# A fixed TensorE order from the second block on, and the first block's weight pairs behind the exponentials, in a windowed attention and two MLPs

## The chip, the cores and the metric

The kernel runs on one NeuronCore of a Trainium2 chip. The metric is the device time of one execution in microseconds. The runs of the kernel before took 1015.44, 1015.37 and 1014.34 us, median 1015.37.

Names used below: PE is TensorE (PEld its weight loads), ACT is ScalarE, DVE is VectorE, POOL is GpSimd, SP is SyncE, whose queue issues the DMAs.

## What is computed

```python
# q, k, v: (4, 8, 576, 64)
scores = scale * np.matmul(q, k.transpose(0, 1, 3, 2))
rel = pos[:, None] - pos[None, :]
mask = (rel >= 0) & (rel < 64)
attn = softmax(where(mask, scores, -1e9))       # in float32
x = np.matmul(attn, v)                          # -> (2304, 512) by token
xn = x / np.sqrt(np.mean(x * x, -1, keepdims=True) + 1e-6) * rms_g
g = xn @ w_gate                                 # 512 -> 1536
x = (g * sigmoid(g) * (xn @ w_val)) @ w_out     # 1536 -> 512
h = x @ w_in                                    # 512 -> 2048
out = (h * sigmoid(1.702 * h)) @ w_out2         # 2048 -> 512
```

## The kernel before

The 2304 tokens are six blocks of 384; a block is three attention tiles of 128 tokens, numbered 0 to 17. A tile is worked on in steps: `att_Tk` and `att_Tq` transpose K and Q on PE and copy them to SBUF; `att_S` computes the scores into two PSUM banks, DVE adds the mask and takes the row minimum, ACT takes eight exponentials, DVE normalises; `att_PT` transposes P; `att_PV` multiplies with V. `rms_sq` squares the result and adds its four parts on DVE, `rms_sum` sums over the partitions on PE and takes the power on POOL, `rms_spread` spreads it on PE and scales x on DVE. `split_x` splits x into two fp32r numbers, `xh` and `xl`.

A projection (`proj`) is twelve matmuls: weight high half by `xh`, low half by `xh`, high half by `xl`, four contraction chunks each. Weights come by DMA as float32 into staging tiles (`st`, three buffers) and are converted pair by pair: `w_step` runs two operations on ACT (lines 163 and 164), then three on DVE (165, 166, 169) that build a rounded number m; `w_half`, at the next step, casts m to the high half on ACT (144) and subtracts on DVE for the low half (145). A pair holds the gate and value weights of one feature chunk, or the output weights of two. The first pass over the six blocks uses the first six feature chunks (nine pairs, 0 to 8), all converted during block 0; the second pass the other six; the second MLP follows.

The opening works off tiles 0 to 2 alone. It has its own PSUM banks and SBUF tiles, and five matmuls of the identity after each transpose (`ps_warm`). Then block 0 begins, and the steps of the later tiles are put between its matmuls: `tick()` counts the matmuls of the projections and accumulations (216 per block), and `due` holds what is to be issued at which count, from the table `score_at` (tile 3 at tick 10, then 42, 74, 112, 202, and every 72).

A scheduler orders each engine's instructions at build time. Where `pinned[0]` is set, PE's instructions keep the order in which the code issues them (`tc.keep_in_program_order`); before, this holds for all blocks of the first pass. `tc.issue_after(ins)` keeps an instruction behind another. `hold[0]` is such an instruction for the two ACT operations of a weight pair: in the opening the last copy, then the split of x, from block 1 on the latest tanh.

The feature loop (lines 601 to 641) runs, per chunk: gate projection, tanh (607) and product (610), value projection, product (614), cast `ah` (617), difference `al` (618), and the accumulation of the chunk before (`emit_O`). `extras` calls `w_step` between them.

Of the kernel before, what the change touches and what calls it, by code (L numbers as in the profile page):

```python
# [22 lines left out]
def window_attention__gated_mlp__mlp_kernel(  # L23
# [28 lines left out]
    T0 = TB  # L52
# [83 lines left out]
    def after(ins):  # L136
        return tc.issue_after(ins) if ins is not None else nullcontext()

    def w_half():
        if not half:  # L140
            return
        pair, w24 = half.pop()
        w = wp.tile([128, 2, 1024], F32R, tag="w", name="w")
        nc.scalar.copy(w[:, 0, :], w24.bitcast(F32))
        nc.vector.tensor_tensor(w[:, 1, :], w24.bitcast(F32), w[:, 0, :].bitcast(F32), ALU.subtract)
        for e, key in enumerate(pair):
            weights[key] = w[:, :, e * 512:(e + 1) * 512]

    def w_step(limit):
        w_half()  # L150
        if w_next[1] >= min(limit, n_w):
            return
        w_load(w_next[1] + 1)
        pair = w_order[w_next[1]]
        w_next[1] += 1
        st = staged.pop(0).rearrange("p e (f two) -> p (e f) two", two=2)
        lo, hi = st[:, :, 0], st[:, :, 1]
        if w_next[1] <= n_wh:
            m = wp.tile([128, 1024], I32, tag="w", name="m")
        else:  # L160
            m = tmp.tile([128, 1024], I32, tag="tmp", name="m")
        with after(hold[0]):
            nc.scalar.mul(hi.bitcast(F32), hi.bitcast(F32), 2.0 ** -112)
            nc.scalar.activation(lo, lo.bitcast(U32), AF.Copy, scale=2.0 ** -29)
        nc.vector.tensor_scalar(m.bitcast(U32), hi.bitcast(U32), 3, None, ALU.logical_shift_left)
        nc.vector.scalar_tensor_tensor(
            m.bitcast(U32), hi.bitcast(U32), 0x80000000, m.bitcast(U32), ALU.bitwise_and, ALU.bitwise_or
        )
        nc.vector.tensor_tensor(m, m, lo, ALU.add)
        half.append((pair, m))  # L170
        w_load(w_next[1] + 2)
# [78 lines left out]

    last_copy = [None]

    def to_sbuf(dst, src, vector=False):
        if vector:
            nc.vector.tensor_copy(dst, src)
        else:
            last_copy[0] = nc.scalar.copy(dst, src).ins

    def att_Tk(m):
        t = ld_tile["k", m]  # L260
        ps = att_bank("k")
        for hp in range(NHP):
            on_pe(nc.tensor.transpose, ps[:, hp * 128:(hp + 1) * 128], t[:, 2 * hp:2 * hp + 2, :], ident)
        s0 = 2 * (m % 2)
        to_sbuf(KT[:, :, s0:s0 + 2, :], ps.rearrange("p (h g t) -> p h g t", h=NHP, g=2), starting[0] and m > 0)
        released(("k", m))

    def att_Tq(m):
# [7 lines left out]
        qts[m] = QT  # L276
        to_sbuf(QT, ps.rearrange("p (h t) -> p h t", h=NHP))
        released(("q", m))
# [9 lines left out]
    def att_S(m):  # L288
# [22 lines left out]
        for e in range(2):  # L311
# [12 lines left out]
            for hp in range(NHP):  # L324
                i = e * NHP + hp
                last_exp[0] = nc.scalar.activation(  # L326
                    p[e][:, hp, :],
                    p[e][:, hp, :],
                    AF.Exp,
                    bias=sm[:, 0, i:i + 1],  # L330
                    scale=-1.0,
                    accum_out=sm[:, 1, i:i + 1],
                ).ins
        for lo, n, pe in [(0, NHP, p[0]), (NHP, NHP, p[1])] if starting[0] else [(0, 2 * NHP, pp)]:
            r = sm[:, 2, lo:lo + n]
# [56 lines left out]
    def rms_sum(x, sq, lo, hi):  # L392
# [24 lines left out]

    def rms_scale(x, sq, lo, hi):
        rms_sum(x, sq, lo, hi)
        return rms_spread(x, lo, hi)  # L420
# [64 lines left out]


    N_ATT = NG // 2
    m0 = TB // 128
    score_at = [0] * m0 + [10, 42, 74, 112] + [202 + 72 * i for i in range(N_ATT - 2 * m0)]

    for fn in (att_Tk, att_Tq):
        at_tick(1, lambda fn=fn: held(fn, m0))
    for m in range(m0, N_ATT):
        b, i = divmod(m, m0)
        t, n = score_at[m], score_at[m + 1] - score_at[m]
        if m == m0:
            at_tick(t, lambda m=m: held(att_S, m))
        else:
            at_tick(t, lambda m=m: att_S(m))
# [4 lines left out]
        at_tick(t + (60 if i == 0 and b > 1 else 48) * n // 72, lambda m=m: att_PT(m, (1,)))  # L504
        pv = t + n + 10
        at_tick(pv, lambda m=m, b=b, i=i: att_PV(m, x_of(b)[0], i * 128))
        at_tick(pv, lambda b=b, i=i: rms_sq(x_of(b)[0], i * 128, x_of(b)[1]))
        if i + 1 == m0:
            at_tick(pv + 24, lambda b=b: rms_sum(*x_of(b), 0, TB))
            at_tick(pv + 38, lambda b=b: rms_spread(x_of(b)[0], 0, TB))  # L510

    if True:
# [52 lines left out]
        for ps_i in range(2):  # L565
            f_lo, f_hi = ps_i * FH, (ps_i + 1) * FH
            for j in range(NB):
                end = j + 1 == NB
                pinned[0] = ps_i == 0
                acc = [acc_p.tile([128, 512], F32, tag=f"acc{c}", name=f"acc{c}") for c in range(KC)]  # L570
# [30 lines left out]
                for f in range(f_lo, f_hi):  # L601
# [14 lines left out]
                    al = ap_.tile([128, TB], F32R, tag="al", name="al")  # L616
                    nc.scalar.copy(ah, a)  # L617
                    nc.vector.tensor_tensor(al, a, ah.bitcast(F32), ALU.subtract)  # L618
# [121 lines left out]
```

## Time and profile before

| what | value |
|---|---|
| median of 3 runs | 1015.37 us |
| the profiled execution's own time | 1013.77 us |
| its span in the profile | 1012.0 us |
| mean granted clock of TensorE | 0.984 |
| PE busy | 975.2 us, 96% |
| DVE, ACT, POOL busy | 51%, 40%, 1% |
| HBM read and written | 68.55 MB and 18.87 MB |

The span is what the profile shows, from the first to the last recorded event; the time is 1.8 us longer. All times in the rows are counted from the start of the span. Busy PE says little of its pace: the granted clock of a stretch (1.00 is 2.4 GHz, 0.50 is 1.2 GHz) has to be read with it.

### The profile page before, as it was taken

Reading aid. Unit: us, or ns where it says so; the run is one execution under the profiler, and the core shown is the slowest. Engines: PE = TensorE matmul, PEld = TensorE weight load, DVE = VectorE, ACT = ScalarE, POOL = GpSimd, SP = SyncE. Lnnn points to the kernel's source line nnn. Section 1 sums busy time; section 2 is a strip of 40 time slices with the busy share of each in tenths; the row PEclk is TensorE's granted clock in tenths of the full one; section 3 lists DMA queues with packets and bytes.
Section 4 is the critical chain, followed back from the end, with each engine's and each line's share of the span. In section 5 each row is a group of like instructions: output and inputs, shape, how many; then the busy total and the mean of one; then the engine's idle time right before and its main releaser. Section 6 shows DMA issues by size and latency. Waiting matters only on the chain.

```text
span 1012.0 us, 15556 instructions
## 1 busy us (share of the span) xinstructions
PE 975.2 (96%) x6200; PEld 914.3 (90%) x6200; DVE 518.6 (51%) x1140; ACT 404.9 (40%) x882; POOL 12.5 (1%) x39
## 2 busy tenths in 40 slices
PE   8569999999999999999999999999999999999997
PEld 7458999989999899999999998998989989989996
DVE  5896657667676654564552788232332322322222
ACT  6687455646563333332332464232222222322222
POOL 2000000000000000000000000000000000000000
PEclk9779999999999999999999999999999999999999
DMA  9866443636443422433421442010010100000000
GB/s 234 215 208 162 112 118 79 175 92 157 116 115 107 158 86 78 136 99 121 135 96 41 136 157 73 1 63 1 1 63 1 45 19 1 32 1 1 32 1 32
DMA packets 113321, 88.44 MB, mean 87 GB/s; under 512 B 77664, under 2 KB 104288, under 8 KB 113248
## 3 DMA queue, kind: packets, MB, share of 16 engines
q1 hardware_dynamic: 112720, 87.44, 29.9%
q8 instruction: 49, 0.80, 0.3%
q14 instruction: 24, 0.20, 0.1%
q10 hardware_dynamic: 528, 0.00, 0.0%
HBM read 68.55 MB, written 18.87 MB: 86 GB/s over the span
## 4 chain that ended last, share of the span: by engine, by line
PE 92%; ACT 2%; DMA 2%; DVE 2%; issue 1%; SPq 0%; POOL 0%; ACTq 0%; DVEq 0%
PE psh L91 20%; PE acc L667 20%; PE acc L91 15%; PE psg L91 14%; PE psv L91 14%; PE ps_v L91 2%; PE ps_s L91 2%; PE ps_t L91 2%; DMA st<-in_moe_w_out_dram 1%; ACT p L326 1%; PE ps_r L91 1%; PE ps_q L91 1%; PE ps_warm L91 1%; PE ps_k L91 1%; DMA o<-x2s 1%
## 5 line engine op out<-in xcount | busy, mean ns | idle before, releaser
L683 DVE TENSOR_TENSOR a<-a,psh 128x384 f32<-128x384 f32 x96 | 53.0, 553 | 202.1 <-ACT a L682 202.1
L91 PE MATMUL psh<-x2h,w 128*128 128x384 f32 x768 | 153.2, 339 | 0.0
L667 PE MATMUL acc<-w,gh 128*128 128x512 f32 x576 | 152.8, 397 | 0.0
L91 PEld LDWEIGHTS psh<-x2h,w 128*128 128x128 f32 x768 | 137.2, 188 | 3.2 <-DVE a L683 0.4
L682 ACT ACTIVATE a<-psh 128x384 f32<-128x384 f32 x96 | 47.0, 491 | 220.4 <-PE psh L91 217.2
L667 PEld LDWEIGHTS acc<-w,gh 128*128 128x128 f32 x576 | 107.0, 188 | 18.5
L91 PE MATMUL acc<-ah,w 128*128 128x384 f32 x576 | 116.4, 342 | 1.9 <-ACT ah L617 1.5
L91 PEld LDWEIGHTS acc<-ah,w 128*128 128x128 f32 x576 | 102.1, 188 | 2.8 <-ACT ah L617 1.8
L91 PE MATMUL psh<-x2l,w 128*128 128x384 f32 x384 | 86.2, 338 | 0.0
L667 PE MATMUL acc<-w,gl 128*128 128x512 f32 x288 | 85.1, 396 | 0.0
L610 DVE SCALAR_TENSOR_TENSOR a<-a,psg 128x384 f32<-128x384 f32 x72 | 39.6, 550 | 83.6 <-ACT a L607 83.6
L687 DVE TENSOR_TENSOR gl<-a,gh 128x384 fp32r<-128x384 f32 x96 | 53.4, 557 | 50.5 <-ACT gh L686 42.7
L607 ACT ACTIVATE a<-psg 128x384 f32<-128x384 f32 x72 | 35.4, 491 | 103.3 <-PE psg L91 103.3
L91 PEld LDWEIGHTS psh<-x2l,w 128*128 128x128 f32 x384 | 69.9, 188 | 5.9
L686 ACT CAST gh<-a 128x384 fp32r<-128x384 f32 x96 | 49.3, 513 | 62.4 <-DVE a L683 49.7
L91 PE MATMUL acc<-al,w 128*128 128x384 f32 x288 | 67.5, 348 | 1.5 <-DVE al L618 1.5
L617 ACT CAST ah<-a 128x384 fp32r<-128x384 f32 x72 | 37.0, 513 | 76.2 <-DVE a L614 75.9
L667 PEld LDWEIGHTS acc<-w,gl 128*128 128x128 f32 x288 | 54.2, 189 | 12.5
L91 PE MATMUL psg<-xh,w 128*128 128x384 f32 x288 | 63.7, 354 | 1.5 <-ACT xh L427 1.5
L326 ACT ACTIVATE p<-p,sm 128x128 f32<-128x128 f32 x128 | 49.6, 389 | 29.0 <-DVE sm L314 29.0
L91 PE MATMUL psv<-xh,w 128*128 128x384 f32 x288 | 60.8, 351 | 0.0
L91 PE MATMUL psv<-x2h,w 128*128 128x384 f32 x288 | 58.9, 340 | 0.0
(108 smaller groups left out, 1415.1 us busy)
## 6 DMA issues: line engine op xcount, KB each, us to landing
st<-in_moe_w_out_dram SPq DMA_DIRECT2D x28, 512.0 KB, 4.3
o<-x2s SPq DMA_DIRECT2D x48, 192.0 KB, 3.8
st<-in_moe_w_in_dram SPq DMA_DIRECT2D x16, 512.0 KB, 4.9
st<-in_moe_w_gate_dram SPq DMA_DIRECT2D x12, 512.0 KB, 4.1
st<-in_moe_w_val_dram SPq DMA_DIRECT2D x12, 512.0 KB, 5.2
qkv<-in_v_dram SPq DMA_DIRECT2D x20, 256.0 KB, 4.0
x<-xraw SPq DMA_DIRECT2D x6, 768.0 KB, 3.3
xr<-x SPq DMA_DIRECT2D x6, 768.0 KB, 4.3
```

Source lines behind the costliest of these rows:

```text
L91: ins = op(*args, **kw)
L326: last_exp[0] = nc.scalar.activation(p[e][:, hp, :], p[e][:, hp, :], AF.Exp, bias=sm[:, 0, i:i + 1], scale=-1.0, accum_out=sm[:, 1, i:i + ...
L607: tanh = nc.scalar.activation(a, psg[:, :T], AF.Tanh, scale=0.5).ins
L610: nc.vector.scalar_tensor_tensor(a, a, 1.0, psg[:, :T], ALU.add, ALU.mult)
L617: nc.scalar.copy(ah, a)
L667: nc.tensor.matmul(acc[c], (gh, gh, gl)[pi][:, c * 128:(c + 1) * 128], w[:, (0, 1, 0)[pi], :], start=(f == 0 and pi == 0), stop=(f == NF2 ...
L682: nc.scalar.activation(a[:, :T], psh[:, :T], AF.Sigmoid, scale=1.702)
L683: nc.vector.tensor_tensor(a[:, :T], a[:, :T], psh[:, :T], ALU.mult)
L686: nc.scalar.copy(gh[:, :T], a[:, :T])
L687: nc.vector.tensor_tensor(gl[:, :T], a[:, :T], gh[:, :T].bitcast(F32), ALU.subtract)
```

## The change

It has these parts:

- `pinned[0]` is set only from block 1 on (`j > 0`), so in block 0 the scheduler orders PE. The tiles 3 to 5 of block 0 are no longer issued at ticks but at `slots`, the calls of `extras` (three per feature chunk); tile 6 and later stay at ticks, from 220 on, at first 48 apart. The normalisation of a block follows its last tile sooner (18 and 30 ticks instead of 24 and 38).
- Weight pairs 1 and 2 wait on ACT for the copy of tile 3's Q, pairs 3 and 4 for tile 3's last exponential, 5 and 6 for tile 4's, 7 and 8 for tile 5's (`gates`, whose key is the pair's number plus one).
- In the opening pair 0 is converted right behind tile 2's last exponential, each operation in two halves of 512 columns.
- In the opening the four parts of the squares are added by PE (four matmuls per tile) instead of two additions on DVE, and each tile is normalised as soon as it is done. K's copies, two of which were DVE's, are all ACT's.
- The split of the next block's input stands behind the last chunk's `ah` and `al`.

```diff
+    def w_cols():
+        return [slice(0, 512), slice(512, 1024)] if starting[0] else [slice(0, 1024)]
...
-        nc.scalar.copy(w[:, 0, :], w24.bitcast(F32))
-        nc.vector.tensor_tensor(w[:, 1, :], w24.bitcast(F32), w[:, 0, :].bitcast(F32), ALU.subtract)
+        for c in w_cols():
+            nc.scalar.copy(w[:, 0, c], w24[:, c].bitcast(F32))
+            nc.vector.tensor_tensor(w[:, 1, c], w24[:, c].bitcast(F32), w[:, 0, c].bitcast(F32), ALU.subtract)
...
-        with after(hold[0]):
-            nc.scalar.mul(hi.bitcast(F32), hi.bitcast(F32), 2.0 ** -112)
-            nc.scalar.activation(lo, lo.bitcast(U32), AF.Copy, scale=2.0 ** -29)
+        for c in w_cols():
+            h, l, mc = hi[:, c], lo[:, c], m[:, c]
+            with after(gates.get(w_next[1], hold[0])):
+                nc.scalar.mul(h.bitcast(F32), h.bitcast(F32), 2.0 ** -112)
+                nc.scalar.activation(l, l.bitcast(U32), AF.Copy, scale=2.0 ** -29)
...
-        to_sbuf(KT[:, :, s0:s0 + 2, :], ps.rearrange("p (h g t) -> p h g t", h=NHP, g=2), starting[0] and m > 0)
+        to_sbuf(KT[:, :, s0:s0 + 2, :], ps.rearrange("p (h g t) -> p h g t", h=NHP, g=2))
...
+        ins = to_sbuf(QT, ps.rearrange("p (h t) -> p h t", h=NHP))
+        if m == T0 // 128:
+            gates[2] = gates[3] = ins
...
+        if 0 <= m - T0 // 128 < 3:
+            for i in range(2):
+                gates[2 * (m - T0 // 128) + 4 + i] = last_exp[0]
...
+        if starting[0]:
+            return s4
...
-            on_pe(nc.tensor.matmul, ms[:, i:i + 1], sq[:, c0:c0 + 128], ones, start=True, stop=True)
+            parts = [sq[:, c0:c0 + 128]] if s4 is None else [s4[:, c, :] for c in range(KC)]
+            for c, part in enumerate(parts):
+                on_pe(nc.tensor.matmul, ms[:, i:i + 1], part, ones, start=(c == 0), stop=(c == len(parts) - 1))
...
-    score_at = [0] * m0 + [10, 42, 74, 112] + [202 + 72 * i for i in range(N_ATT - 2 * m0)]
+    score_at = [220, 268, 316, 364, 433, 502, 572, 642, 712, 784, 856, 928, 1000]
...
+        s0, lags = 1 + 4 * i, (2, 3, 4, 5, 5, 6)
...
+    at_slot(0, s0 + lags[5], lambda: rms_sum(*x_of(1), 0, TB))
+    for fn in (att_Tk, att_Tq):
+        at_slot(0, s0 + lags[5], lambda fn=fn: fn(2 * m0))
+    at_slot(0, s0 + lags[5], lambda: rms_spread(x_of(1)[0], 0, TB))
...
-            at_tick(pv + 24, lambda b=b: rms_sum(*x_of(b), 0, TB))
-            at_tick(pv + 38, lambda b=b: rms_spread(x_of(b)[0], 0, TB))
+            at_tick(pv + 18, lambda b=b: rms_sum(*x_of(b), 0, TB))
+            at_tick(pv + 30, lambda b=b: rms_spread(x_of(b)[0], 0, TB))
...
+        hold[0] = last_exp[0]
+        w_step(1)
         ps_warm = [acc_p.tile([128, 512], F32, tag="acc3", name="ps_warm")]
         for m in range(T0 // 128):
             att_PT(m)
-            if m + 1 == T0 // 128:
-                hold[0] = last_copy[0]
-                w_step(1)
             att_PV(m, x, m * 128)
-            rms_sq(x, m * 128, sq)
-        for m in range(T0 // 128):
-            pe_hold = rms_scale(x, sq, m * 128, (m + 1) * 128)
+            s4 = rms_sq(x, m * 128, sq)
+            pe_hold = rms_scale(x, sq, m * 128, (m + 1) * 128, s4)
+        w_half()
...
-                pinned[0] = ps_i == 0
+                pinned[0] = ps_i == 0 and j > 0
...
-                        split_x(x, nxh, nxl, T)
+                        with after(ah_ins), after(al_ins):
+                            split_x(x, nxh, nxl, T)
```

Three places in the order of instructions. ACT, start of block 0, before (`st` are the staged pairs 1 to 3, `KT` and `QT` the copies of tile 3's K and Q):

```order
L427 CAST xh_552<-xraw_215 128x384 x2
L163 ACTIVATE st_117<-st_117 128x1024
L164 ACTIVATE st_117<-st_117 128x1024
L163 ACTIVATE st_122<-st_122 128x1024
L164 ACTIVATE st_122<-st_122 128x1024
L163 ACTIVATE st_577<-st_577 128x1024
L164 ACTIVATE st_577<-st_577 128x1024
L257 COPY KT_93<-ps_k_582 128x4x128
L257 COPY QT_92<-ps_q_590 128x512
```

The same place in the changed kernel:

```order
L438 CAST xh_565<-xraw_215 128x384
L259 COPY KT_93<-ps_k_597 128x4x128
L438 CAST xh_565<-xraw_215 128x384
L259 COPY QT_92<-ps_q_605 128x512
L169 ACTIVATE st_117<-st_117 128x1024
L170 ACTIVATE st_117<-st_117 128x1024
L169 ACTIVATE st_122<-st_122 128x1024
L170 ACTIVATE st_122<-st_122 128x1024
L148 CAST w_679<-m_613 128x1024
```

Tile 3's copies moved in front of all pairs of block 0, and pair 3 behind pairs 1 and 2.

ACT around tile 4's exponentials (`p_798`), with the pairs 5 (`st_750`) and 6 (`st_827`) and chunk 2's tanh (line 639), in the changed kernel:

```order
L330 ACTIVATE p_798,sm_797<-p_798,sm_797 128x128 x8
L169 ACTIVATE st_750<-st_750 128x1024
L170 ACTIVATE st_750<-st_750 128x1024
L169 ACTIVATE st_827<-st_827 128x1024
L639 ACTIVATE a_843<-psg_830 128x384
L170 ACTIVATE st_827<-st_827 128x1024
L381 COPY xraw_846<-ps_v_848 128x4x128
```

Before, there stood (tile 4's exponentials, `p_765`, behind the first operations of the pair `st_1028`; `a_736` is chunk 1's):

```order
L144 CAST w_1019<-m_899 128x1024
L607 ACTIVATE a_736<-psg_709 128x384
L163 ACTIVATE st_1028<-st_1028 128x1024
L164 ACTIVATE st_1028<-st_1028 128x1024
L144 CAST w_1118<-m_1022 128x1024
L326 ACTIVATE p_765,sm_764<-p_765,sm_764 128x128 x8
L257 COPY KT_93<-ps_k_791 128x4x128
```

The pairs moved from ahead of a tile's exponentials to behind them, and a tanh came to stand behind weight operations.

PE, the spread of the normalisation for block 1 (`ps_r<-ident,ry`), before, in the middle of block 0:

```order
L91 MATMUL acc_566<-ah,w 128x384
L91 MATMUL acc_567<-ah,w 128x384
L91 MATMUL ps_r<-ident,ry 128x128 x3
L91 MATMUL acc_564<-ah,w 128x384
L91 MATMUL acc_565<-ah,w 128x384
```

In the changed kernel, at the end of block 0:

```order
L91 MATMUL acc_577<-al,w 128x384
L91 MATMUL acc_578<-al,w 128x384
L91 MATMUL acc_579<-al,w 128x384
L91 MATMUL acc_580<-al,w 128x384
L91 MATMUL ps_r<-ident,ry 128x128 x3
L91 MATMUL psg<-xh,w 128x384 x4
L91 MATMUL ps_s<-KT,QT 64x128 x16
```

The spread moved behind the last accumulation of block 0, directly in front of block 1's first projection.

## Rows read from the trace of the kernel before

**Rows 1.** The page: the span, and busy time of the engines.

```profile
span 1012.0 us, 15556 instructions
PE 975.2 (96%) x6200; PEld 914.3 (90%) x6200; DVE 518.6 (51%) x1140; ACT 404.9 (40%) x882; POOL 12.5 (1%) x39
```

**Rows 2.** Stretches: length, busy time per engine (instructions); PE's clock, DMA share, GB/s.

```profile
21.90:38.17 16.27, 9.43 (x108) 8.13 (x108) 10.36 (x28) 8.51 (x15) 1.99 (x3) 0.84 0.85 212
38.17:80.00 41.83, 27.04 (x185) 23.91 (x186) 39.83 (x80) 36.32 (x69) 0.00 (x0) 0.70 0.78 219
80.00:122.45 42.45, 42.44 (x405) 39.22 (x405) 26.56 (x89) 23.55 (x76) 0.86 (x1) 0.99 0.45 120
122.45:175.60 53.15, 52.10 (x468) 49.45 (x467) 34.55 (x103) 28.83 (x80) 0.85 (x1) 1.00 0.45 110
```

**Rows 3.** Waits of PE, 38.1 to 80 us: total, times, longest.

```profile
PE ps_t L91 <- DVE p L338: 4.7, 1, 4.7
...
PE ps_q L91 <- ACT KT L257: 3.2, 1, 3.2
PE ps_s L91 <- ACT QT L257: 2.5, 1, 2.5
```

**Rows 4.** Timeline, opening's end: start, length, engine, operation, [idle before <- releaser].

```profile
29.71 0.63 ACT L386 ACTIVATE quad<-xraw 128x512 f32<-128x512 f32 x1
...
32.85 0.80 PE L91 MATMUL ps_r<-ones,sq 128*128 128x1 f32 x4 [3.40 <-DVE sq L388]
...
36.20 2.15 DVE L413 SCALAR_TENSOR_TENSOR xraw<-xraw,g_sb,ps_r 128x128 f32<-128x128 f32 x8 [1.47 <-PE ps_r L91]
...
38.17 0.69 PE L91 MATMUL psg<-xh,w 128*128 128x384 f32 x1 [1.49 <-ACT xh L427]
```

**Rows 5.** Timeline of PE around the end of block 0.

```profile
117.55 1.10 PE L91 MATMUL ps_s<-KT,QT 64*64 64x128 f32 x32
118.58 0.62 PE L91 MATMUL acc<-al,w 128*128 128x384 f32 x2
...
120.55 1.15 PE L91 MATMUL ps_v<-pt,qkv 128*64 128x64 f32 x32
121.63 0.98 PE L91 MATMUL acc<-al,w 128*128 128x384 f32 x4
122.45 0.60 PE L91 MATMUL ps_k<-ident,qkv 128*128 128x128 f32 x4
122.80 1.66 PE L91 MATMUL psg<-xh,w 128*128 128x384 f32 x8
...
125.00 0.60 PE L91 MATMUL ps_q<-ident,qkv 128*128 128x128 f32 x4
```

**Rows 6.** Groups by shape, 36.7 to 122.5 us: busy, mean ns, idle before.

```profile
L166 DVE SCALAR_TENSOR_TENSOR m<-st,m 128x1024 uint32<-128x1024 uint32 x8 | 9.8, 1222 | 0.1
...
L145 DVE TENSOR_TENSOR w<-m,w 128x1024 fp32r<-128x1024 f32 x8 | 9.7, 1214 | 0.5 <-ACT w L144 0.5
...
L314 DVE CUSTOM_DVE_ANT_0 p<-ps_s,masks 128x128 f32<-128x128 f32 x40 | 8.8, 286 | 0.7 <-PE ps_s L91 0.7
...
L165 DVE TENSOR_SCALAR m<-st 128x1024 uint32<-128x1024 uint32 x8 | 5.5, 690 | 0.0
...
L338 DVE TENSOR_TENSOR p<-p,sm 128x1024 f32<-128x1024 f32 x4 | 4.9, 1218 | 0.0
...
L614 DVE TENSOR_TENSOR a<-a,psv 128x384 f32<-128x384 f32 x6 | 3.3, 550 | 2.3 <-PE psv L91 2.3
...
L413 DVE SCALAR_TENSOR_TENSOR xraw<-xraw,g_sb,ps_r 128x384 f32<-128x384 f32 x4 | 2.2, 608 | 0.0
```

**Rows 7.** Timeline of DVE: the low half of pair 8.

```profile
84.50 1.23 DVE L145 TENSOR_TENSOR w<-m,w 128x1024 fp32r<-128x1024 f32 x1 [0.45 <-ACT w L144]
```

**Rows 8.** Short stretches: length, PE busy; PE's clock, DMA share, GB/s.

```profile
72.20:74.70 2.50, 2.47 (x40) 1.00 0.99 329
77.80:80.70 2.90, 2.81 (x10) 0.50 1.24 251
```

**Rows 9.** Timeline of PE ahead of the first of them.

```profile
71.89 0.63 PE L91 MATMUL ps_k<-ident,qkv 128*128 128x128 f32 x4 [1.56 <-issue]
```

More of the change, by code (lines that the diff above doesn't have):

```diff
@@ L161, in w_step @@
             m = tmp.tile([128, 1024], I32, tag="tmp", name="m")
-        with after(hold[0]):
-            nc.scalar.mul(hi.bitcast(F32), hi.bitcast(F32), 2.0 ** -112)
-            nc.scalar.activation(lo, lo.bitcast(U32), AF.Copy, scale=2.0 ** -29)
[L165 to L169, printed above, removed]
+        for c in w_cols():
[3 more added lines that the diff above has]
+                nc.scalar.activation(l, l.bitcast(U32), AF.Copy, scale=2.0 ** -29)
+            nc.vector.tensor_scalar(mc.bitcast(U32), h.bitcast(U32), 3, None, ALU.logical_shift_left)
+            nc.vector.scalar_tensor_tensor(
+                mc.bitcast(U32), h.bitcast(U32), 0x80000000, mc.bitcast(U32), ALU.bitwise_and, ALU.bitwise_or
+            )
+            nc.vector.tensor_tensor(mc, mc, l, ALU.add)
         half.append((pair, m))
@@ L232, in window_attention__gated_mlp__mlp_kernel @@
     hold = [None]
+    gates = {}
     starting = [True]
@@ L249, in att_bank, with to_sbuf @@
         return atp.tile(shape, F32, tag="att", name="ps_" + kind)
[L251 to L257, printed above, removed]
+    def to_sbuf(dst, src):
+        return nc.scalar.copy(dst, src).ins
     def att_Tk(m):
@@ L276, in att_Tq @@
         qts[m] = QT
-        to_sbuf(QT, ps.rearrange("p (h t) -> p h t", h=NHP))
+        ins = to_sbuf(QT, ps.rearrange("p (h t) -> p h t", h=NHP))
+        if m == T0 // 128:
+            gates[2] = gates[3] = ins
         released(("q", m))
@@ L390, in window_attention__gated_mlp__mlp_kernel, with rms_sum @@
     rms_r = {}
-    def rms_sum(x, sq, lo, hi):
+    def rms_sum(x, sq, lo, hi, s4=None):
         n = (hi - lo) // 128
@@ L416, in rms_spread, with rms_scale @@
         return mm.ins
-    def rms_scale(x, sq, lo, hi):
-        rms_sum(x, sq, lo, hi)
+    def rms_scale(x, sq, lo, hi, s4=None):
+        rms_sum(x, sq, lo, hi, s4)
         return rms_spread(x, lo, hi)
@@ L466, in x_store, with at_slot @@
         nc.sync.dma_start(out=xd[j], in_=x)
+    NS = 3 * FH
+    slots = {}
     xs = {}
+    def at_slot(j, s, fn):
+        slots.setdefault(j * NS + s, []).append(fn)
     def x_of(b):
@@ L488, in window_attention__gated_mlp__mlp_kernel @@
     m0 = TB // 128
-    score_at = [0] * m0 + [10, 42, 74, 112] + [202 + 72 * i for i in range(N_ATT - 2 * m0)]
+    score_at = [220, 268, 316, 364, 433, 502, 572, 642, 712, 784, 856, 928, 1000]
     for fn in (att_Tk, att_Tq):
-        at_tick(1, lambda fn=fn: held(fn, m0))
-    for m in range(m0, N_ATT):
-        b, i = divmod(m, m0)
[L495 to L499, printed above, removed]
+        at_slot(0, 0, lambda fn=fn: held(fn, m0))
+    for i in range(m0):
+        m = m0 + i
+        s0, lags = 1 + 4 * i, (2, 3, 4, 5, 5, 6)
+        if i == 0:
+            at_slot(0, s0, lambda m=m: held(att_S, m))
+        else:
+            at_slot(0, s0, lambda m=m: att_S(m))
+        if i + 1 < m0:
+            at_slot(0, s0 + lags[0], lambda m=m + 1: att_Tk(m))
+            at_slot(0, s0 + lags[1], lambda m=m + 1: att_Tq(m))
+        at_slot(0, s0 + lags[2], lambda m=m: att_PT(m))
+        at_slot(0, s0 + lags[3], lambda m=m, i=i: att_PV(m, x_of(1)[0], i * 128))
+        at_slot(0, s0 + lags[4], lambda i=i: rms_sq(x_of(1)[0], i * 128, x_of(1)[1]))
+    at_slot(0, s0 + lags[5], lambda: rms_sum(*x_of(1), 0, TB))
+    for fn in (att_Tk, att_Tq):
+        at_slot(0, s0 + lags[5], lambda fn=fn: fn(2 * m0))
+    at_slot(0, s0 + lags[5], lambda: rms_spread(x_of(1)[0], 0, TB))
+    for m in range(2 * m0, N_ATT):
+        b, i = divmod(m, m0)
+        t, n = score_at[m - 2 * m0], score_at[m - 2 * m0 + 1] - score_at[m - 2 * m0]
+        at_tick(t, lambda m=m: att_S(m))
         if m + 1 < N_ATT:
@@ L503, in window_attention__gated_mlp__mlp_kernel @@
         at_tick(t + 44 * n // 72, lambda m=m: att_PT(m, (0,)))
-        at_tick(t + (60 if i == 0 and b > 1 else 48) * n // 72, lambda m=m: att_PT(m, (1,)))
+        at_tick(t + (60 if i == 0 and b > 2 else 48) * n // 72, lambda m=m: att_PT(m, (1,)))
         pv = t + n + 10
@@ L588, in extras @@
                     if ps_i == 0:
+                        for fn in slots.pop(j * NS + s, ()):
+                            fn()
                         if j == 0:
@@ L616, in window_attention__gated_mlp__mlp_kernel @@
                     al = ap_.tile([128, TB], F32R, tag="al", name="al")
-                    nc.scalar.copy(ah, a)
-                    nc.vector.tensor_tensor(al, a, ah.bitcast(F32), ALU.subtract)
+                    ah_ins = nc.scalar.copy(ah, a).ins
+                    al_ins = nc.vector.tensor_tensor(al, a, ah.bitcast(F32), ALU.subtract).ins
                     if f == f_hi - 1 and ps_i == 0 and not end:
```

## The prediction

> **What bounds the kernel now.** I read the page first, then the table of stretches, the waits of the stretch that stands out, and last the timeline around its two ends. The page shows TensorE (PE) busy for 975.2 us, 96% of the span [rows 1]: whatever the change gives must come out of the other 37 us, or out of stretches in which PE was busy at its lower clock. The table of stretches [rows 2] says where these are. From 122.45 us on PE is busy for 52.1 of 53.2 us per block at granted clock 1.00, so there is almost nothing to win there. Between 38.17 and 80.00 us it is busy for 27.0 of 41.8 us, at a mean clock of 0.70, while VectorE (DVE) is busy for 39.8 of the 41.8 us: here DVE, which turns packed weights into pairs of fp32r halves, is the bound. Between 21.90 and 38.17 us, the tail of the opening, PE is busy for 9.4 of 16.3 us. From 80.00 to 122.45 us PE is the bound again (42.4 of 42.5 us), working off what it could not do earlier.
>
> The waits of the bad stretch [rows 3] are PE waiting for a softmax (4.7 us), for ScalarE (ACT) to copy K and Q out of PSUM (3.2 and 2.5 us), and for the split input (1.5 us). They hurt because before the change PE's order in the first block is the written one: a transpose that waits for its softmax holds up projections that are ready.
>
> **The times that the sum starts from.** The first matmul of the first block starts at 38.17 us, after a wait for the split [rows 4]. The first block's last accumulating matmuls start at 121.63 us, the second block's first projection at 122.80, and that projection is over at 125.00 [rows 5]. From the same rows: one set of four transposes takes 0.35 us (122.45 to 122.80), the scores of a tile 1.03 (117.55 to 118.58), the product with V 1.08 (120.55 to 121.63), and a projection 2.12 at the full clock (122.80 to 125.00, less what lies between its two parts). On DVE one pair of weights costs 0.69 + 1.22 + 1.22 + 1.21 = 4.35 us (the row of line 166 stands for 169 too); a feature chunk three operations of 0.55; a tile 1.22 for the scaling, 0.4 for sums and reciprocals, and eight score operations of 0.29, which start 0.21 apart: 3.3 us [rows 6].
>
> **Term 1, the opening.** Before, the last square ends at 30.34 us, but its two additions stand on DVE behind pair 0's conversion; PE waits 3.4 us and starts the row sums at 32.85 [rows 4]. In the changed kernel PE adds the four parts, so DVE's additions go. And the change moves pair 0's first operations ahead, onto ACT right behind the last exponential, in halves of 512. That is the price: four half operations at 0.63 (taken from the 512 wide square [rows 4], since a half conversion does not occur before) stand in front of the copies of the transposed P. ACT then has 2.5 us of halves and ten operations of the same width (4 copies of P, 3 of outputs, 3 squares) at about 0.6, 8.5 us in all, after the last exponential at about 21.4 (K's two copies moved to ACT, DVE free earlier: about 0.5 sooner than now). With 1.3 us of waits for PE in between, the last square ends at 31.2, later than now by 0.9. From there: row sum 0.45; the reciprocal root's first step waits on DVE behind eight scalings (2.15 us [rows 4]) and a weight half, until 33.6; POOL and spread about 1.5; then the next tile's two sets of transposes, which now stand in front, at twice 0.35 while the clock is low, with scaling and cast of the first chunk beside them. First projection: 36.6, **1.6 us earlier**. Bounds: 35.3 (no waits on ACT) to 39.0 (four halves as dear as the 1024 wide 1.22 of rows 6, 2.4 more); I take the square's price, whose width and engine are the same.
> The Trainium skill (ScalarE: Activation LUTs, Rules for kernel authors) budgets about 0.3 us per instruction and 0.83 ns per element, so a half would take 0.73 us, not 0.63; by it the term would be 1.2 instead of 1.6 us.
>
> **Term 2, the first block.** The order view shows the price of gating the pairs: pairs 3 and 4 (counting from 0) stand on ACT behind tile 3's exponentials, 5 and 6 behind tile 4's, 7 and 8 behind tile 5's, and each feature chunk's tanh and cast stand among them. I went down the three queues of the changed program by hand, row by row, with the durations of rows 4 to 6. DVE's work from 36.4 us until pair 8's second half: 2.9 (split) + 8 x 4.35 + 3 tiles x 3.3 + 5 chunks x 1.65 + 1.4 (squares) = 57.3 us. Its waits: 0.5 us for chunk 1's cast, behind pairs 3 and 4 on ACT; 1.3 for tile 4's exponentials, behind two weight casts; 4.4 for tile 5's scores, which PE issues at 86 us because chunk 2's tanh stands behind three weight operations on ACT and PE idles 4.4 us for it from 67.5; 0.5 for tile 5's exponentials; some 2.6 in small ones. Sum 66.6: pair 8 is ready at about 103 us, against 85.7 before (84.50 + 1.23 [rows 7]). PE has then still some 8 us to do, part of it at the low clock after an idle stretch of 5 us (93 to 98), so its last accumulating matmuls end at about 110.5 us, not 122.45: 12 us earlier. But it has done less by then. Against the point 125.00 us of before, two and a half sets of tile work are still owed: P transposes 0.72, V 1.08, two sets of transposes 0.70, scores 1.03, the next K's 0.35: **3.9 us**.
>
> **Term 3, the border to the second block.** Before, that block's input was normalised in the middle of block 0 (tick 160 of 216). In the changed order the three spread matmuls stand behind PE's very last accumulating matmul, so the chain is bare: spread 0.5, four scalings at 0.61 (2.4), casts and subtractions of the four chunks on DVE and ACT about 3. The first projection of block 1 with the scores beside it needs 3.2 us of PE and is over at about 117.3, 6.8 after the 110.5: a stall of 3.6 us. Compared at the end of this projection: 125.00 - 117.3 - 3.9 = **3.8 us gained**; term 1 is in it.
>
> **Edits at nothing.** The ordering of the split behind the last cast costs nothing: 24 accumulating matmuls (4.2 us) follow it on PE. The tiles of blocks 1 to 4 come at other ticks, but PE does the same work there and was 98% busy [rows 2]; tile 6 to 8 at 48 ticks instead of 72 leave about 7 us from scores to transposes where 5.6 are needed; without that cover it is up to 1 us per tile. K's copies on ACT lie beside exponentials. No DMA is added; the weight loads still follow the release of their staging buffer, and with the pairs gated they are issued earlier before use (pair 4: at 42 for 55 us).
>
> So the span becomes 1012.0 - 3.8 = 1008.2. The profiled run took 1013.77 us, 1.6 under the median of 1015.37; the same difference on the median gives **1011.6 us**.
>
> **Rival A, the low clock (slower).** PE's clock: after a gap of 1.56 us it was at 1.00, after one of 3.2 us [rows 3] at 0.50 [rows 8, 9]. The changed order leaves PE gaps of 2.1, 2.4, 4.4 and 5 us in block 0. I charged only the last two. If the first two also count, a projection takes 4.3 instead of 2.12 us; two of them stand in front of chunk 1's product on DVE, in whose queue tile 3's scaling and pairs 3 and 4 wait: 2 x 2.2 there, and 2.2 + 1 at the same place for chunk 3 and 5, 7.5 us: 1019 us. It decides from the point at which a gap of some 2 us lowers the clock. For it: before, the mean clock of the whole stretch was 0.70, with gaps of 2.5 to 4.7 us in it [rows 2, 3]; against it: the first burst of the changed block is longer and denser than any of those.
> The Trainium skill says the same as a rule (TensorE: Matmul & The Clock Gate, HAM oscillation): gaps put the array back to its throttled state and each burst after them starts cold. By that rule alone, with each of the four gaps counted, the time would be that of this rival; the trace agrees for 3.2 us and not for 1.56.
>
> **Rival B, DVE stays full (faster).** Before, DVE idled for 2.0 of 41.8 us. If in the freed order PE issues tile 5's scores in time, the idle falls from 9.3 to about 2 and pair 8 is ready 7.3 us earlier: 1004.3 us. Against it: the order is fixed at build time, and ACT's queue shows chunk 2's tanh behind the weights.
>
> **Rival C, no change.** The bare normalisation is not only at block 1: block 2's spread stands at tick 404, its split at 408 of 432 (before, 394). If each of a few borders loses 1 us or the dense tiles of block 1 stall, 3.8 becomes 1 to 2: 1014 us.
>
> **How the numbers follow.** My sum 0.50, A 0.20, B 0.16, C 0.14. The sum is good to 3 us (bounds of term 1: 1.3 less and 2.4 more, of the waits about 2.5). From 1004 to 1019 it takes in the sum, C, and about half of A and B. A measurement of this kernel tells about 0.2% (2.0 us) from no change: faster needs less than 1013.3, which holds for B and 0.7 of the sum: 0.52; the same: C and a quarter of the sum, 0.26; slower: A and the sum's rest, 0.22.
>
> **What would show it.** Right: the first projection near 36.6 us, pair 8's last operation near 103, the spread matmuls behind the last accumulating ones near 110, then a PE gap. Rows at 0.50 granted clock between 44 and 57 would show A; DVE above 95% busy until 97 us, B; gaps at each later border, C. A block 0 that ends after 119 us, or before 103, proves the queue reading wrong.

## The result, and the profile after

The changed kernel takes 1019.99 us (median of 5 runs, 1018.66 to 1023.55), the kernel before beside it 1014.52 (1014.03 to 1015.44): a ratio of 1.0056, 95% interval 1.0039 to 1.0073. It is slower by 0.6%; the prediction was 1011.6 us, between 1004 and 1019. A second series of the changed kernel gave 1021.6 us and 1.0065.

The profiled execution is the slowest of the five, 1023.55 us. The page, for [rows 1]:

```profile
span 1021.8 us, 15582 instructions
PE 983.9 (96%) x6218; PEld 918.9 (90%) x6218; DVE 516.3 (51%) x1136; ACT 407.9 (40%) x887; POOL 13.0 (1%) x39
```

DVE and ACT did the same work within 3 us. PE shows 8.7 us more, though no large work was added. Why is not settled: the rows below show matmuls at the lower clock, but the mean granted clock of the two executions is nearly the same (0.982, and 0.984 before). The table of stretches for [rows 2] (length, busy PE, PEld, DVE, ACT, POOL; granted clock, DMA share, GB/s), cut at the events of the new order:

```profile
37.10:80.00 42.90, 35.43 (x251) 32.34 (x250) 38.27 (x81) 33.17 (x70) 0.00 (x0) 0.86 0.65 192
80.00:97.60 17.60, 13.22 (x124) 11.31 (x122) 11.06 (x30) 11.64 (x29) 0.00 (x0) 0.89 0.36 100
97.60:110.10 12.50, 12.50 (x91) 11.93 (x92) 6.79 (x11) 4.43 (x8) 0.86 (x1) 0.88 0.76 212
110.10:120.40 10.30, 8.07 (x56) 6.54 (x56) 7.40 (x28) 5.16 (x21) 0.00 (x0) 0.70 0.52 180
120.40:175.00 54.60, 53.26 (x495) 49.68 (x498) 36.32 (x106) 33.30 (x90) 0.86 (x1) 0.99 0.46 113
```

PE is fuller than before up to 80 us (35.4 of 42.9, not 27.0 of 41.8), and then there is a hole that was not there: between 80.0 and 97.6 us PE is idle for 4.4 us and DVE for 6.5. PE's timeline at the places that the prediction named (start, length, operation, [idle before <- what ended it]):

```profile
37.10 0.67 PE L91 MATMUL psg<-xh,w 128*128 128x384 f32 x1
...
46.05 2.93 PE L91 MATMUL psg<-xh,w 128*128 128x384 f32 x8 [1.98 <-DVE a L642]
...
71.63 2.93 PE L91 MATMUL psg<-xh,w 128*128 128x384 f32 x8 [3.92 <-DVE a L642]
...
95.65 1.11 PE L91 MATMUL ps_t<-ident,p 128*128 128x128 f32 x4 [2.62 <-ACT xraw L381]
...
109.49 0.94 PE L91 MATMUL acc<-al,w 128*128 128x384 f32 x4
110.28 0.83 PE L91 MATMUL ps_r<-ident,ry 128*128 128x128 f32 x6
112.36 0.44 PE L91 MATMUL psg<-xh,w 128*128 128x384 f32 x1 [1.25 <-ACT xh L438]
113.66 1.43 PE L91 MATMUL psg<-xh,w 128*128 128x384 f32 x3 [0.86 <-DVE xh L436]
115.02 1.99 PE L91 MATMUL ps_s<-KT,QT 64*64 64x128 f32 x32
116.93 1.65 PE L91 MATMUL psg<-xh,w 128*128 128x384 f32 x4
118.38 1.48 PE L91 MATMUL psg<-xl,w 128*128 128x384 f32 x4
```

And DVE's, around its longest wait and at pair 8:

```profile
86.66 0.29 DVE L318 CUSTOM_DVE_ANT_0 p<-ps_s,masks 128x128 f32<-128x128 f32 x1 [5.16 <-PE ps_s L91]
...
101.79 1.23 DVE L149 TENSOR_TENSOR w<-m,w 128x1024 fp32r<-128x1024 f32 x1 [1.11 <-ACT w L148]
```

Block 0 came out as forecast: first projection at 37.1 us (forecast 36.6), pair 8 ready at 103.0 (103), last accumulating matmuls over at 110.4 (110.5). That is 12 us earlier than before. The kernel is slower all the same, so the time is lost behind it. The tanh of chunk 0 (line 639, before 607) marks where a block begins. Its starts for blocks 1 to 5, read from ACT's timeline, in us:

| kernel | block 1 | 2 | 3 | 4 | 5 |
|---|---|---|---|---|---|
| before | 125.3 | 178.7 | 232.1 | 285.4 | 334.4 |
| the change | 120.5 | 183.4 | 240.5 | 293.9 | 344.6 |
| the change, another execution (1018.13 us) | 120.1 | 180.7 | 234.9 | 288.0 | 339.2 |

Ahead by 5 us at block 1, behind by 2 to 5 at block 2. Some of this is work still owed, which the change moved from block 0 to block 1 (tile 6's scores from tick 112 to 220, and so on). The rest shows at the borders. The waits of PE, as in [rows 3] but between 130 and 400 us, in the changed kernel:

```profile
PE psg L91 <- DVE a L642: 6.3, 3, 3.0
PE acc L91 <- ACT ah L649: 2.3, 2, 1.3
PE ps_t L91 <- DVE p L345: 1.2, 2, 1.1
```

The first row is new: three waits for the product that frees the PSUM tile of the gate projection. The longest is at the border from block 1 to 2. All engines there, in the changed kernel:

```profile
173.77 0.49 ACT L684 ACTIVATE x2s<-acc 128x384 f32<-128x384 f32 x1
...
174.29 7.00 SPq L685 DMA_DIRECT2D o<-x2s  x4
...
174.37 1.10 PE L91 MATMUL ps_s<-KT,QT 64*64 64x128 f32 x32
...
179.92 0.49 ACT L684 ACTIVATE x2s<-acc 128x384 f32<-128x384 f32 x1 [5.66 <-DMA o<-x2s]
180.31 0.39 ACT L330 ACTIVATE p<-p,sm 128x128 f32<-128x128 f32 x1
...
183.01 0.39 ACT L330 ACTIVATE p<-p,sm 128x128 f32<-128x128 f32 x1
183.39 0.47 ACT L639 ACTIVATE a<-psg 128x384 f32<-128x384 f32 x1
183.89 0.55 DVE L642 SCALAR_TENSOR_TENSOR a<-a,psg 128x384 f32<-128x384 f32 x1
184.50 0.44 PE L91 MATMUL psg<-xh,w 128*128 128x384 f32 x1 [3.01 <-DVE a L642]
```

The same border before the change:

```profile
169.82 1.10 PE L91 MATMUL ps_s<-KT,QT 64*64 64x128 f32 x32
...
173.29 0.40 ACT L326 ACTIVATE p<-p,sm 128x128 f32<-128x128 f32 x1 [3.24 <-DVE sm L314]
...
176.38 0.47 ACT L651 ACTIVATE x2s<-acc 128x384 f32<-128x384 f32 x1
...
178.69 0.48 ACT L607 ACTIVATE a<-psg 128x384 f32<-128x384 f32 x1
...
182.38 0.49 ACT L651 ACTIVATE x2s<-acc 128x384 f32<-128x384 f32 x1 [2.74 <-DMA o<-x2s]
```

`x2s` is the copy of a finished block's result, four pieces, alternately by ACT and DVE, through two staging tiles. So ACT's second copy must wait until the DMA of the first piece has landed, 5.66 us in the changed kernel. Before, tile 10's scores stood at tick 418, and its eight exponentials and the tanh were done by the time ACT stood at that copy: the wait cost nobody anything. The change puts the scores at tick 433, one tick behind the border at 432. Now the copy stands in front, and the exponentials, the tanh, the product and PE's next projection queue behind it. Over all borders ACT waits for these DMAs about as long as before (12.3 us between 130 and 400 us, before 13.3); what stands behind the wait is new.

The four pieces of 192 KB took 1.9 to 5.5 us from issue to landing, 2.9 in the median. The slow one was issued behind two weight loads of 512 KB (at 172.0 and 172.4 us), the second of which took 6.9 us to land. That these loads make it slow is argued from the order of the times; no run moves them.

Theory 1 was therefore that the ticks of tiles 10 to 17 are the loss (the table `score_at`), with the rivals that the copies alone, or PE's free order in block 0, make it.

### The profile page after: what moved, and what is told of

Same layout as the page of the kernel before. It is cut to its first block, busy times and chain, and to the rows that moved or that the text cites. A ratio compares the mean times of both kernels' runs of the same rounds, so it can differ in the third digit from the quotient of the medians.

```text
span 1021.8 us, 15582 instructions
## 1 busy us (share of the span) xinstructions
PE 983.9 (96%) x6218; PEld 918.9 (90%) x6218; DVE 516.3 (51%) x1136; ACT 407.9 (40%) x887; POOL 13.0 (1%) x39
## 4 chain that ended last, share of the span: by engine, by line
PE 84%; DVE 7%; ACT 5%; DMA 3%; issue 1%; SPq 0%; POOL 0%; ACTq 0%; DVEq 0%
PE acc L700 20%; PE psh L91 20%; PE psg L91 14%; PE psv L91 13%; PE acc L91 12%; DMA o<-x2s 2%; ACT p L330 1%; PE ps_s L91 1%; PE ps_v L91 1%; DVE m L172 1%; DVE xraw L424 1%; PE ps_t L91 1%; PE ps_r L91 1%; ACT st L169 1%; DVE m L175 1%
## 5 line engine op out<-in xcount | busy, mean ns | idle before, releaser
L91 PE MATMUL acc<-ah,w 128*128 128x384 f32 x576 | 116.9, 341 | 3.0 <-ACT ah L649 3.0
L91 PE MATMUL psg<-xh,w 128*128 128x384 f32 x288 | 68.4, 370 | 14.9 <-DVE a L642 12.2
L91 PEld LDWEIGHTS psg<-xh,w 128*128 128x128 f32 x288 | 54.0, 202 | 19.1 <-DVE a L642 13.7
L91 PE MATMUL psv<-xh,w 128*128 128x384 f32 x288 | 65.8, 356 | 0.0
L91 PE MATMUL acc<-al,w 128*128 128x384 f32 x288 | 64.3, 342 | 0.8 <-DVE al L650 0.8
L330 ACT ACTIVATE p<-p,sm 128x128 f32<-128x128 f32 x128 | 49.6, 389 | 31.0 <-DVE sm L318 30.8
```

The costliest lines, as they stand in the source:

```text
L91: ins = op(*args, **kw)
L330: last_exp[0] = nc.scalar.activation(p[e][:, hp, :], p[e][:, hp, :], AF.Exp, bias=sm[:, 0, i:i + 1], scale=-1.0, accum_out=sm[:, 1, i:i + ...
```

## The experiments

All were run in rounds beside the kernel before (1014.6 to 1015.1 us in the median of its runs); the ratio is against it.

### The change again

> The changed kernel as it is, again, for the same chip as the others. Both theories: 1.004 to 1.007 of the kernel before, 1018 to 1021 us. Its trace again has PE waits for chunk 0's product at the start of blocks 2, 3 and 4 (3.0, 2.0 and 1.3 us).

Measured: 1021.6 us (1018.13 to 1023.25, 6 runs), ratio 1.0065 (1.0051 to 1.008). The loss is real. Its profiled run is the fastest of the series, 5.4 us below the profile above, of the same program. The two differ in the clock at the borders: there the wait for the product was 2.37 us and the clock stayed at 1.00 from 183 to 186 us; above, it was 3.01 us, and the short stretches behind it show

```profile
184.50:187.00 2.50, 2.50 (x13) 2.48 (x14) 2.13 (x5) 1.45 (x3) 0.00 (x0) 0.78 1.20 225
187.00:190.00 3.00, 3.00 (x13) 2.97 (x12) 1.07 (x2) 0.49 (x1) 0.00 (x0) 0.61 0.41 78
```

One long wait thus costs itself and, in some executions, more at the lower clock behind it: at full clock the work of these 5.5 us would have taken 3.8 (an estimate, 2.50 x 0.78 + 3.00 x 0.61).

### The ticks of before for tiles 10 to 17

```diff
-    score_at = [220, 268, 316, 364, 433, 502, 572, 642, 712, 784, 856, 928, 1000]
+    score_at = [220, 268, 316, 364, 418, 490, 562, 634, 706, 778, 850, 922, 994]
```

> The change with the ticks of tiles 10 to 17 as before (418, 490, ... 922), 6 to 15 ticks earlier. Theory 1 (the loss is at the borders of blocks 1 to 4, where a tile's scores now stand within 8 ticks of the border, so that its exponentials and the next tanh stand on ACT behind an output copy that waits for a DMA): the three waits of PE for chunk 0's product go, 5 to 7 us less than the change, 1012 to 1015 us. Rival (the loss is in block 0, from the gated pairs): 0 to 2 us less.

Measured: 1014.09 us (1010.87 to 1014.83, 11 runs), ratio 0.9988 (0.9979 to 0.9997): 6 to 7.5 us less than the change. No wait for the product is left between 130 and 400 us. What stands there:

```profile
PE ps_v L91 <- issue: 4.8, 3, 1.7
PE acc L91 <- DVE al L650: 1.3, 1, 1.3
```

This row with `ps_v` is in the kernel before too, 1.04 us at each of three places. The ticks are the loss; without them the change is worth half a microsecond. That is less than the 3.8 I had summed, so something in block 0 or at its end must be off as well.

### More copies on DVE

```diff
-                    elif c % 2:
+                    elif c:
```

> The change with three of the four output copies of the first pass on DVE and one on ACT, so that ACT's exponentials stand behind no copy that waits for a DMA. Theory 1: ACT's idle of 5.7 us before the third copy goes, but DVE then waits for the same DMA ahead of half of the scores; 1 to 4 us less than the change. Rival (the loss is in block 0): within 1 us of the change.

Measured: 1019.55 us (1014.93 to 1022.81, 10 runs), ratio 1.0039 (1.0025 to 1.0053), about 2 us less than the change with its own ticks. The profiled run is the fastest of the ten; in it PE waits 1.2 us for the product, not 4.5 to 6.3. Taking ACT out of the wait helps, but then DVE, which has to give the product, stands in it: at the border from block 1 its second copy starts at 175.76 us, when the first piece has landed (171.0 + 4.7), after 1.75 us of idle time in the middle of the scores. By the medians this recovers a third at most; what the slower executions lose, this trace does not show.

### The ticks of the change in the kernel before

```diff
-    score_at = [0] * m0 + [10, 42, 74, 112] + [202 + 72 * i for i in range(N_ATT - 2 * m0)]
+    score_at = [0] * m0 + [10, 42, 74, 112] + [202, 274, 346, 433, 502, 572, 642, 712, 784, 856, 928, 1000]
```

> The kernel before, with nothing changed but the ticks of tiles 10 to 17 (418, 490, 562 and so on become 433, 502, 572 and so on, the ticks of the change). Theory 1 (a tile whose scores stand at a block's border has its exponentials behind the output copy that waits for a DMA; this is the loss): 1014.7 plus 6 to 7 us, about 1021, and PE waits for the product of line 610 at the borders after blocks 1, 2 and 3, 4 to 7 us in all between 130 and 400 us. Theory 2 (the ticks hurt only together with the shorter first block of the change): within 1.5 us of 1014.7.

Measured: 1023.12 us (1022.82 to 1025.79, 4 runs), ratio 1.0088 (1.0074 to 1.0102). The ticks alone cost 8.3 us, somewhat more than in the change. PE waits for the product at two borders, not at the three expected. The waits of PE between 130 and 400 us:

```profile
PE acc L91 <- ACT ah L617: 4.5, 3, 2.7
PE psg L91 <- DVE a L610: 3.9, 2, 3.1
```

At the border from block 1 the chain is the one above, line by line: ACT's second copy held 3.02 us by its DMA, eight exponentials, the tanh, the product, and PE's projection behind a wait of 3.13 us.

### Only the border's tiles back

```diff
-    score_at = [220, 268, 316, 364, 433, 502, 572, 642, 712, 784, 856, 928, 1000]
+    score_at = [220, 268, 316, 364, 418, 502, 572, 634, 712, 784, 850, 928, 1000]
```

> The changed kernel, gates and all, where only the three tiles whose scores stand at a block's border go back to the ticks of before (10, 13 and 16: 433, 642, 856 become 418, 634, 850); the other five keep the change's ticks. Theory 1 (the loss is that of scores at the border, behind the output copies' DMA): about 1014, as with all ticks back. Theory 2 (the loss comes from all the later ticks, by products and normalisation that stand later in each block): 1017 to 1021.

Measured: 1017.25 us (1015.1 to 1019.65, 12 runs), ratio 1.0022 (1.0012 to 1.0032). Between the two theories: 3 to 4 of the 6 to 7.5 us come back with the three border tiles, and no wait for the product of line 642 is left. The rest stays with the other five ticks; PE's waits ahead of the product with V grow to 2.46 us at one place, where all ticks of before give 1.71. All waits of PE between 130 and 400 us add up to 6.5 us in the kernel before, 7.0 with all ticks back, 9.4 here, and 12.6 and 10.9 in the two executions of the change. So the rest is in waits again, none of them for that product; why these five ticks cause them is open.

### A fixed order of PE in block 0

```diff
-                pinned[0] = ps_i == 0 and j > 0
+                pinned[0] = ps_i == 0
```

> The change with PE's order fixed in block 0 too, so that the spread of block 1's normalisation stands in the middle of chunk 5, not at the border. Theory 1: the border wait of 2.2 us and the low clock behind it go, but PE in block 0 stalls for softmaxes again: 3 us less to 3 us more than the change. Rival (block 0's loss comes from the gates, not from PE's order): the same within 1 us.

Measured: 1018.75 us (1018.33 to 1020.68, 5 runs), ratio 1.0044 (1.0032 to 1.0056): the free order does not help the change; fixed, it is 1 to 3 us faster. With the ticks of before:

> The changed kernel with the ticks of before for tiles 10 to 17 and with PE's order fixed in block 0 too. Theory 1 (the two edits act at different places and add: 6.5 us for the ticks, 2.5 for the order): about 1011.6, faster than the kernel before by 0.3%. Theory 2 (what the fixed order gave stands in the stretch that the ticks recover anyway): 1014, as with the ticks alone.

Measured: 1009.28 us (1008.98 to 1011.69, 5 runs), ratio 0.9949 (0.9936 to 0.9963). That is 4.8 us below the same ticks with the free order, more than either theory said. PE at the end of block 0, with the free order and the ticks of before:

```profile
110.29 0.94 PE L91 MATMUL acc<-al,w 128*128 128x384 f32 x4
111.08 0.83 PE L91 MATMUL ps_r<-ident,ry 128*128 128x128 f32 x6
...
118.93 0.87 PE L91 MATMUL psg<-xl,w 128*128 128x384 f32 x4
```

and with the fixed order:

```profile
109.93 0.87 PE L91 MATMUL acc<-al,w 128*128 128x384 f32 x4
110.64 0.87 PE L91 MATMUL psg<-xh,w 128*128 128x384 f32 x4
...
113.28 0.87 PE L91 MATMUL psg<-xl,w 128*128 128x384 f32 x4
```

Block 0 ends within half a microsecond of the same place, but block 1's first projection is over at 119.6 us with the free order and at 114.0 with the fixed one. The fixed order has the spread of the normalisation in the middle of block 0 again (102.45 us), so the border is not bare: 3.3 us from the last accumulating matmul to the end of the projection, not 8.6. Ahead of the border the order gains next to nothing.

### The opening alone

The kernel before with the half weights (pair 0 right behind tile 2's exponentials), the row sums of four parts on PE and K's copies on ACT; ticks and order of before, no gates, no slots. Three places of the edit:

```diff
+        for c in w_cols():
...
-        to_sbuf(KT[:, :, s0:s0 + 2, :], ps.rearrange("p (h g t) -> p h g t", h=NHP, g=2), starting[0] and m > 0)
+        to_sbuf(KT[:, :, s0:s0 + 2, :], ps.rearrange("p (h g t) -> p h g t", h=NHP, g=2))
...
+            pe_hold = rms_scale(x, sq, m * 128, (m + 1) * 128, s4)
```

> The kernel before with the opening of the change alone (half weights, row sums of four parts on PE, K's copies on ACT); block 0, its order and all ticks are those of before. Theory 1 (the opening gives what its first projection is earlier, 38.17 to about 37.1 us, and DVE, the bound of block 0, starts earlier too): 1 us less, about 1013.6. Theory 2 (block 0 is bound by pair conversions on DVE, of which the half weights only move the first, so the opening's gain goes into a wait): 1014.7.

Measured: 1014.18 us (1013.42 to 1015.27, 11 runs), ratio 0.9997 (0.9988 to 1.0005): nothing that can be told from no change. Chunk 0's tanh of block 0 comes 1.6 us earlier than before (49.6 for 51.2), chunk 0's of block 1 only 0.2 earlier (125.1 for 125.3). In between the lead shrinks from 1.6 us to 0.6 at chunk 2 and 0.2 at chunk 3 (84.2 for 84.9, 95.3 for 95.5): it is used up in the stretch that DVE bounds.

### Without the gates

With the ticks of before, and all weight pairs of block 0 free of their gates:

```diff
-            with after(gates.get(w_next[1], hold[0])):
+            with after(hold[0]):
```

> The changed kernel with the ticks of before for tiles 10 to 17, and the weight pairs of block 0 no longer gated by the tiles' exponentials. Theory 1 (gating holds DVE for the tiles and is what ends block 0 earlier): block 0 ends later than 110 us, and the time is 1016 or more. Theory 2 (PE's 4.4 us and 5 us gaps in block 0 come from the gating, and its gain is taken back at the border): 1011 to 1014, no worse than with the gates.

Measured: 1006.16 us (1004.2 to 1007.68, 5 runs), ratio 0.9916 (0.9903 to 0.9928), the fastest version found, 7.9 us below the same kernel with gates. Two stretches of each, with the gates:

```profile
60.00:80.00 20.00, 15.98 (x128) 14.90 (x128) 17.54 (x37) 14.40 (x32) 0.00 (x0) 0.83 0.73 212
80.00:93.00 13.00, 11.75 (x116) 10.56 (x115) 6.71 (x25) 6.43 (x21) 0.00 (x0) 1.00 0.26 81
```

and without:

```profile
60.00:80.00 20.00, 17.25 (x145) 15.71 (x133) 19.07 (x41) 15.69 (x34) 0.00 (x0) 1.00 0.72 208
80.00:93.00 13.00, 12.71 (x113) 12.19 (x114) 11.78 (x31) 8.95 (x26) 0.00 (x0) 0.87 0.55 154
```

DVE, the third busy column after the length, is busy for 30.9 of 33 us, not 24.3. Its timeline and PE's in the kernel without gates (pair 8's low half, and the first projection of block 1):

```profile
90.79 1.22 DVE L149 TENSOR_TENSOR w<-m,w 128x1024 fp32r<-128x1024 f32 x1
...
106.27 0.44 PE L91 MATMUL psg<-xh,w 128*128 128x384 f32 x1 [1.25 <-ACT xh L438]
```

Pair 8 is ready at 92.0 us, not 103.7 (102.45 and 1.23 in the kernel with gates and these ticks), because the last pairs no longer wait for tile 5, whose scores waited for a tanh that stood behind gated weight operations.

### Only pairs 1 and 2 gated

```diff
-                gates[2 * (m - T0 // 128) + 4 + i] = last_exp[0]
+                pass
```

> The changed kernel with the ticks of before for tiles 10 to 17, where only pairs 1 and 2 are gated (behind the copy of tile 3's Q) and pairs 3 to 8 are free. Theory 1 (the exponentials' gates are what holds DVE and ACT back, since pair 8 waits for tile 5): near 1006, as without gates. Theory 2 (the late pairs 1 and 2 start a chain that the rest inherits): near 1014, as with all gates.

Measured: 1010.82 us (1010.69 to 1011.57, 5 runs), ratio 0.996 (0.9947 to 0.9974), between the two: of 7.9 us the exponentials' gates make 3.3, the one on pairs 1 and 2 the other 4.7. Pair 8 is ready at 93.0 us here, so the 11 us by which it comes sooner are worth 3.3, but PE waits 2.2 and 1.7 us for weight halves at 45.8 and 54.5 us.

### No gates, the change's own ticks; and no gates, fixed order

The edit that takes the gates out, on the change itself; and on the kernel without gates and with the ticks of before, the order fixed in block 0:

```diff
-                pinned[0] = ps_i == 0 and j > 0
+                pinned[0] = ps_i == 0
```

> The changed kernel, its own ticks kept, with only the gates of the weight pairs in block 0 taken out. Theory 1 (gates and ticks act at different places and add; the gates cost 8 us, as without them at the ticks of before): about 1012.5. Theory 2 (the ticks' loss grows when block 0 ends earlier, or the gates' loss is felt only where the borders don't stall): 1016 to 1021.

Measured: 1010.95 us (1010.61 to 1012.65, 5 runs), ratio 0.9963 (0.995 to 0.9975): the gates alone turn the change from 0.6% slower to 0.4% faster, 9 to 10.7 us. With the ticks of before another 4.8 us go, so the two costs nearly add; the ticks cost 6 to 7.5 with the gates.

> No gates, ticks of before for tiles 10 to 17, and PE's order fixed in block 0 too. Theory 1 (a fixed order takes 4.8 us off, as it did with the gates): about 1001.5. Theory 2 (the fixed order only repaired what the gates had made of PE's order, so that nothing is left for it): 1005 to 1008, or more where a fixed order makes PE wait for a late tile again.

Measured: 1011.51 us (1011.14 to 1012.1, 5 runs), ratio 0.9965 (0.9953 to 0.9978), 5.4 us slower than with the free order. The time is that of theory 2, which allowed for waits behind a late tile. The waits of PE from 36 to 125 us:

```profile
PE ps_t L91 <- DVE p L345: 5.7, 3, 4.0
PE ps_s L91 <- ACT pt L259: 3.4, 3, 2.4
```

A fixed order waits for a late softmax, as before the change [rows 3]; a free order goes past it. Without gates the free order therefore ends block 0 at 102.1 us, 8.5 ahead of the fixed one (110.6), and can pay the bare border, 10.7 us to the end of the first projection, not 3.3. With the gates and the ticks of before it has no such lead (111.1 for 110.6), because products behind gated weights cost it 5.7 us in this stretch, and only the price of the border is left. No run has both, a free order without gates and the normalisation ahead of the border.

## Why the prediction was wrong

- **Term 1, the opening:** right in the trace (37.1 us for 36.6, 38.17 before [rows 4]), and worth nothing by itself, as the opening alone shows. The four half operations took 0.67 to 0.68 us each, above my 0.63, but started 0.56 apart, so that they held ACT for 2.3 us and not 2.5. The 0.73 by the Trainium skill (ScalarE: Activation LUTs, Rules for kernel authors) is a budget for operations whose bias comes through a pointer, and these have constants.
- **Term 2, the first block:** its events are right to half a microsecond: PE's wait at 71.6 us was 3.9 (forecast 4.4 from 67.5), tile 5's scores reached DVE at 86.7 (86), pair 8 stood at 103.0, block 0 ended at 110.4. The owed work was priced too low. From the end of block 1's first projection to the end of block 2's first, PE was busy for 57.65 us with 553 matmuls in the changed kernel with the ticks of before, in the same stretch before for 52.33 with 469. The 84 more are just the sets that the sum names, but they took 5.3 us, not 3.9, at a clock of 1.00 in both; why is not settled.
- **Term 3, the border:** forecast 117.3 us for the end of the first projection. At the full clock (the second execution) the next matmul starts at 117.9; in the profile above at 119.7, because after the waits of 1.25 and 0.86 us the scores and two thirds of the projection ran at the lower clock (1.99 us for 1.10, 1.65 and 1.48 for 0.97 and 0.87). I had charged the border no clock. Of 3.8 us, 125.0 - 117.9 - 5.3 = 1.8 were left at best and 0.0 in the other execution; the runs with the ticks of before show 0.6 in the median. At the full clock the border was as forecast, 7.0 us from the last accumulating matmul for my 6.8, but a price that the change need not have paid: with the order fixed it takes 3.3 us.
- **The step that failed is "Edits at nothing"**: "The tiles of blocks 1 to 4 come at other ticks, but PE does the same work there and was 98% busy". The sentence counts PE's work, which was indeed the same. It did not ask what stands on ACT at those ticks. The change's ticks put three tiles' scores at a border, behind a copy that waits for a DMA; the ticks cost 6 to 7.5 us here, 8.3 in the kernel before and 4.8 without gates, against nothing, or "up to 1 us per tile" for other tiles and another reason. The border's three tiles are shown to make about half of it; how the other five ticks lose the rest is open.
- **Rival A, the low clock:** a gap of 1.98 us did bring half the clock (46.05 us, eight matmuls in 2.93), one of 1.32 in the second execution did not. But block 0 ended when forecast, so its 7.5 us were not lost at its place. The time came near 1019 for another reason, by luck. By the Trainium skill's rule (TensorE: Matmul & The Clock Gate, HAM oscillation) a wait that is long enough puts the clock back and the next burst starts cold; the trace agrees for 3.92 and 1.98 us, and not for the 2.37 us at the border in the second execution.
- **Rival B, DVE full,** fell for the change, and its figure came out near without the gates, when DVE was busy 30.9 of 33 us: 1006.2 us, for a forecast of 1004.3. That is in part luck: an earlier pair 8 was worth 3.3 us, not 7.3, and the rest came from pairs 1 and 2. I had read the gates' cost correctly (a tanh behind the weights) and counted it as part of a gain, not as the largest single thing that the change could leave out.
- **Rival C** looked at the borders, but at the normalisation (block 2's split at tick 408), not at the copies at tick 432, and priced a microsecond for each.

The sum, then, against 1014.6 us: block 0 and its border -0.6, the ticks +6 to +7.5, in all 1020 to 1021.5. It meets the measured time by construction, since the ticks' price is the difference between the change and the same kernel with the ticks of before; with the 8.3 us that the kernel before gave on its own it would be 1022.3.

## What to carry to other kernels

When a table moves work to another place in a loop, look at each engine's queue at the new place, not only at the work: the copy that waits for a DMA cost nothing here as long as what stood behind it was not needed, and cost PE 3 us at one border as soon as something short and urgent (exponentials, a tanh) came to stand behind it. Tying one stream of work behind another to protect it (here weights behind exponentials) should be tried without the tie: here it cost 8 us, because the streams met again on one engine's queue. Whether a fixed order helps depends on such ties and on what it leaves bare at a border, so they are tried together.

## What had not been expected of the hardware

The clock after a short wait is not the same from one execution to the next: in the same program, the same place had a wait of 3.01 us and a clock of 0.61 to 0.78 behind it, or 2.37 us and 1.00; the border of block 0, with the same two waits of about 1.25 and 0.86 us, was followed by 0.50 (116.9 to 119.6 us) in one execution and by 1.00 (116 to 120 us) in the other. The changed kernel's runs spread over 5 us, 1018.1 to 1023.6, and in the records of two series the longest have a lower mean clock than the shortest (0.982 at 1023.3 and 1023.6 us, 0.991 at 1018.1), though not run by run (0.989 at 1021.6). Whether more waits make a kernel less steady, these runs do not show: with the most waits, the ticks of the change in the kernel before, four runs lay within 3 us.
